# Seven block products instead of eight for half of the hidden features, from batch 2 on

## The chip, the cores and the metric

The kernel runs on one core of one Trainium2 chip. The metric is device microseconds of one execution; less is better. The kernel before took 519.63 us, the median of three runs (519.27 to 521.14).

The core's engines work side by side, each on a queue of its own in a fixed order: TensorE (PE, matrix products, results in the eight PSUM banks), VectorE (DVE), ScalarE (ACT), GpSimd (POOL, which works on SBUF tiles only here) and SyncE (SP), which issues the DMAs.

## The reference, cut to what matters

```
a    = softmax(phi over the sequence)              # per batch and head, 576 x 32
k_m  = einsum('bhsm,bhsd->bhmd', a, k);  v_m = einsum('bhsm,bhsd->bhmd', a, v)
attn = softmax(scale * q @ k_m^T) @ v_m            # 8 batches, 8 heads, 576 tokens, 64 wide
x    = attn, heads side by side                    # 4608 x 512
a, b = x @ w1, x @ w2                              # 512 -> 1024 each
out  = ((a * b) @ w3) @ w_out                      # 1024 -> 1024 -> 512
```

The inputs are float64 words, which the kernel turns into fp32 itself; it works at fp32 accuracy.

## The kernel before, in words

The product w3 @ w_out is made once. Per batch, `v_m` is multiplied into w1 and w2 (`memory_weights`, tokens M0 to M3, one for each quarter of 256 of the 1024 features), so that a and b come from the probabilities directly: the inner dimension is 256 (8 heads x 32 memory slots), in two blocks t of 128. Every operand is split into a high and a low part of reduced width, and a product is three matmuls: high by high, high by low, low by high.

A batch has three stages on PE:

- **a and b** (`ab_unit`, L589). For each half n of the tokens (288) and each f of eight blocks of 128 features, one unit: a in one PSUM bank, b in another, each 2 blocks t x 3 = 6 matmuls of 128x288, so 12 a unit and 16 units, 192 matmuls, a batch. Then ScalarE copies a out of its bank (L609, token `a`), and VectorE multiplies b by it into g (L612, token `g`).
- **sums of g** on GpSimd (L618, L630, L632, L634; tokens f and S), as the out stage already runs on Strassen's scheme in Winograd's form.
- **out** (`out_unit`, L654, token `O`): 14 units of 12 matmuls (L668). For each, ScalarE makes the high part (L646, token h) and VectorE the low part (L652, token l).

The attention of the next batches runs beside this: the softmax of the token scores (scc, mx, sb, ex, sm, mu, tr: L289 to L317), the high and low part of the probabilities `at` (ah L322, al L326), and the matmuls for memories, scores and M (L227, L277, L350), with Mh (ScalarE, L361) and Ml (VectorE, L369).

The order on every engine is written out by hand. The strings FIRST (batch 0), SECOND (batch 1) and BATCH (batches 2 to 7) are lists of tokens, and each engine's queue holds its instructions in the order of the tokens. An engine that reaches an instruction whose input isn't there waits, with all that is queued behind it.

PSUM has four banks `ab` (two pairs, handed out from the list `free_banks`), one pair `o` and one pair `x`. A unit of a and b takes a pair; the bank of a is handed back by ScalarE's copy, the bank of b by VectorE's multiply. So the third unit of a stage needs the first one's multiply.

The SBUF tiles that matter: `ph` (phi transposed), `a` (phi by tokens), `kv0`, `kv2`, `kv4`, `q`, `s_sb` (scores), `at`, one buffer each; `sh` and `sl` (four each), `c` (three).

Of the kernel before, what the change touches and what calls it, by code (L numbers as in the profile page):

```python
# [33 lines left out]
f3 s2 E3 bm g g bs w1 y1 h2 A a A D0 t2 g l2 Et1 E0 S2 z2 be mem A exp norm D1 E1 memc a a l0 g g block O blockc w0
y0 h1 l1 h4 h3 t3 l4 t1 z1 z3 M0 sc0 scc0 mx0 sb0 O O l3 O O Mh0 h6 S3 S1 l6 h5 Ml0 l5 O S4 h7 p4 p1 h11 ex0 l7 O O
h9 h8 C11 sm0 mu0 tr0 l8 sc1 q2 M1 l9 O u2 ah0 h10 l10 O h12 p5 Mh1 h13 scc1 l11 al0 l12 l13 O O O O C21 C22 Ml1 mx1
sb1 ex1 C12 sm1
# [3 lines left out]
be a g A a A mem norm memc g phi2 l0 a A block g a blockc A M0 kv2 a +top g sc0 M1 g scc0 Mh1 f1 h1 A f3 mx0 sb0 A a
f2 a Ml1 ex0 g g sm0 Mh0 A +bm Ml0 a A O a A g h3 h2 +bs l1 g M2 a mu0 l3 +exp +be g sc1 Mh2 S3 l2 M3 scc1 mx1 S2 h4
+mem Ml2 O S1 l4 h5 +norm O p1 O O sb1 ex1 l5 h6 O Mh3 +memc h8 sm1 h7 S4 u2 l6 h9 tr0 O l7 l8 C11 h10 l9 l10 O p5 O
h11 h12 mu1 +block ah0 O O l11 al0 tr1 h13 l13 l12 O q2 C22 C12 +blockc Ml3 ah1 O O al1 C21
# [14 lines left out]
def memory_attention__then__bilinear_ffn_kernel(  # L59
# [84 lines left out]
    def load_phi(b):  # L144
        t = att.tile([P, NT, S], F32, name="ph", tag="ph")
        nc.sync.dma_start(out=t, in_=phiT[b].rearrange("t p s -> p t s"))
        a = att.tile([P, 9 * P], F32, name="a", tag="a")
# [1 line left out]
        loaded["ph", b] = t, a

    def load_kv(b):
        t = []
        for i in range(0, 4, 2):
# [693 lines left out]
```

## Time and profile before

| | |
|---|---|
| median of three runs | 519.63 us |
| the profiled execution | 520.16 us, its span 518.4 us |
| granted TensorE clock | 0.999 of 2.4 GHz |
| PE / DVE / ACT / POOL busy | 507.8 / 383.8 / 279.9 / 149.6 us |

The span runs from the first to the last instruction; 1.8 us of the execution lie around it. Busy time counts the stretches in which at least one instruction of an engine was under way. A matmul's own duration (about 295 ns) overlaps the next one's, so the pace of PE is read from the chain of waits, where a run of matmuls stands with its count.

### The profile page before, as it was taken

What the parts mean: (1) busy time and instruction counts of PE and PEld (TensorE: products, weight loads), DVE (VectorE), ACT (ScalarE), POOL (GpSimd) and SP (SyncE); (2) the same over time, 40 slices, a digit from 0 to 9 for tenths busy, and PEclk for the clock granted to TensorE, in tenths of its full rate; (3) what the DMA queues carried; (4) which work ended last, traced back from release to release, by engine and by line L of the source; (5) the groups of instructions that cost most, each with busy time, mean ns of one, the idle gap of its engine ahead of it and who ended that gap; (6) DMA issues with size and microseconds to landing.
All of it is one profiled execution on the core that took longest, in us unless ns stands there. A gap on an engine that the chain in (4) does not pass through costs nothing.

```text
span 518.4 us, 10996 instructions
## 1 busy us (share of the span) xinstructions
PE 507.8 (98%) x4488; PEld 443.3 (86%) x4488; DVE 383.8 (74%) x647; ACT 279.9 (54%) x494; POOL 149.6 (29%) x158
## 2 busy tenths in 40 slices
PE   7998999999999999999999999999999999999997
PEld 6344459899788998989988998999898989899996
DVE  4878989889869985769566976688577936893363
ACT  6876989864436643645364625373355425543352
POOL 0005005763020801163023602080207111721280
PEclk9999999999999999999999999999999999999999
DMA  8999943603853048004810263006600400010002
GB/s 280 413 406 362 387 172 108 227 1 127 283 189 136 1 161 296 1 2 138 290 31 1 92 229 138 2 4 207 248 1 1 162 24 1 0 60 34 2 3 91
DMA packets 29795, 68.87 MB, mean 133 GB/s; under 512 B 1840, under 2 KB 10032, under 8 KB 29744
## 3 DMA queue, kind: packets, MB, share of 16 engines
q1 hardware_dynamic: 29744, 68.16, 36.9%
q8 instruction: 35, 0.57, 0.5%
q14 instruction: 16, 0.13, 0.1%
HBM read 58.72 MB, written 9.44 MB: 131 GB/s over the span
## 4 chain that ended last, share of the span: by engine, by line
PE 93%; DMA 3%; DVE 1%; issue 1%; ACT 1%; SPq 0%; ACTq 0%; DVEq 0%
PE ab L600 40%; PE o L668 19%; PE x L668 10%; PE ab L668 5%; PE ab L350 3%; PE x L502 3%; PE x L227 3%; DMA raw<-in_w_out 2%; PE o L502 2%; PE ab L502 2%; PE o L350 1%; PE x L350 1%; PE ab L277 1%; DMA raw<-in_w3T 1%; PE x L277 1%
## 5 line engine op out<-in xcount | busy, mean ns | idle before, releaser
L600 PE MATMUL ab<-ah,mh 128*128 128x288 f32 x512 | 152.5, 298 | 0.0
L600 PE MATMUL ab<-al,mh 128*128 128x288 f32 x512 | 151.1, 295 | 1.0 <-DVE al L326 1.0
L600 PE MATMUL ab<-ah,ml 128*128 128x288 f32 x512 | 151.0, 295 | 0.0
L612 DVE TENSOR_TENSOR g<-ab,a_sb 128x288 f32<-128x288 f32 x128 | 57.6, 455 | 71.2 <-PE ab L600 66.3
L609 ACT COPY a_sb<-ab 128x288 f32<-128x288 f32 x128 | 51.2, 401 | 99.5 <-PE ab L600 96.3
L600 PEld LDWEIGHTS ab<-ah,mh 128*128 128x128 f32 x512 | 96.2, 188 | 8.2 <-issue 5.7
L600 PEld LDWEIGHTS ab<-al,mh 128*128 128x128 f32 x512 | 96.3, 188 | 1.5 <-DVE al L326 1.2
L600 PEld LDWEIGHTS ab<-ah,ml 128*128 128x128 f32 x512 | 96.2, 188 | 0.0
L652 DVE TENSOR_TENSOR sl<-g,sh 128x576 fp32r<-128x576 f32 x98 | 83.2, 873 | 6.8 <-ACT sh L646 6.6
L618 POOL TENSOR_TENSOR g<-g,g 128x288 f32<-128x288 f32 x32 | 29.6, 932 | 200.1 <-DVE g L612 200.1
L646 ACT CAST sh<-g 128x576 fp32r<-128x576 f32 x98 | 65.4, 678 | 33.9 <-PE o L668 14.0
L668 PE MATMUL o<-sh,Wh 128*128 128x288 f32 x248 | 74.0, 298 | 0.0
L668 PE MATMUL o<-sh,Wl 128*128 128x288 f32 x248 | 73.2, 295 | 0.0
L668 PE MATMUL o<-sl,Wh 128*128 128x288 f32 x248 | 73.1, 295 | 0.0
L630 POOL TENSOR_TENSOR q<-g,g 128x288 f32<-128x288 f32 x28 | 22.2, 819 | 101.4 <-PE x L277 91.5
L668 PEld LDWEIGHTS o<-sh,Wh 128*128 128x128 f32 x248 | 46.6, 188 | 4.9 <-issue 4.4
L668 PEld LDWEIGHTS o<-sh,Wl 128*128 128x128 f32 x248 | 46.7, 188 | 0.0
L668 PEld LDWEIGHTS o<-sl,Wh 128*128 128x128 f32 x248 | 46.6, 188 | 0.0
L668 PE MATMUL x<-sl,Wh 128*128 128x288 f32 x136 | 40.1, 295 | 0.0
L668 PE MATMUL x<-sh,Wl 128*128 128x288 f32 x136 | 40.1, 295 | 0.0
L668 PE MATMUL x<-sh,Wh 128*128 128x288 f32 x136 | 40.0, 294 | 0.0
L634 POOL TENSOR_TENSOR g<-g,q 128x288 f32<-128x288 f32 x28 | 34.9, 1275 | 0.0
(132 smaller groups left out, 887.2 us busy)
## 6 DMA issues: line engine op xcount, KB each, us to landing
kv<-in_kv SPq DMA_DIRECT2D x16, 1024.0 KB, 9.4
q<-in_qT SPq DMA_DIRECT2D x8, 1152.0 KB, 5.5
outT<-c SPq DMA_DIRECT2D x31, 288.0 KB, 2.4
raw<-in_w3T SPq DMA_DIRECT2D x6, 1024.0 KB, 11.4
ph<-in_phiT SPq DMA_DIRECT2D x8, 576.0 KB, 5.0
a<-in_phi_tok SPq DMA_DIRECT2D x8, 576.0 KB, 5.9
raw<-in_w SPq DMA_DIRECT2D x4, 1024.0 KB, 15.5
kv<-in_w SPq DMA_DIRECT2D x3, 1024.0 KB, 14.3
```

What stands on the lines that cost most here:

```text
L227: nc.tensor.matmul(ps[t][h * M : (h + 1) * M, : 2 * D], lhsT=v["a"][:, (NT * i + t) * P + h * M : (NT * i + t) * P + (h + 1) * M], rhs=kvt ...
L350: nc.tensor.matmul(ps[t][g * M : (g + 1) * M], lhsT=vm[b % 2][d, g], rhs=w12_sb[q][d, :, g], start=True, stop=True,)
L502: nc.tensor.matmul(pw[r][i][:, cols], lhsT=x[:, i * P : (i + 1) * P], rhs=wos[k // half][:, k % half, cols], start=k == 0 and cols.start == 0,
L600: nc.tensor.matmul(banks[w][:, :HALF], lhsT=x[:, t, w, fc : fc + P], rhs=y[:, n, t * HALF : (t + 1) * HALF], start=i == 0, stop=i == len(t ...
L609: nc.scalar.copy(out=a_sb, in_=banks[0][:, :HALF])
L612: nc.vector.tensor_tensor(out=G[n, f // half][:, f % half], in0=banks[1][:, :HALF], in1=a_sb, op=ALU.mult)
L618: nc.gpsimd.tensor_tensor(out=low, in0=top, in1=low, op=ALU.subtract)
L630: gp(out=s2, in0=a22, in1=s3, op=ALU.subtract)
L634: gp(out=a12, in0=a12, in1=s2, op=ALU.subtract)
L646: nc.scalar.copy(out=hi, in_=src)
L652: nc.vector.tensor_tensor(out=lo, in0=src, in1=hi.bitcast(F32), op=ALU.subtract)
L668: nc.tensor.matmul(ps[j][:, :HALF], lhsT=piece(x, s, 2 * part + k)[:, jc], rhs=y[:, k], start=i in first and part == 0 and k == 0 and t == ...
```

## The change

In batches 2 to 7 the last two quarters of the features (f 4 to 7) are no longer made by `ab_unit`. A quarter's a and b together are, for each of w1 and w2, a product of 2 x 2 blocks (2 feature blocks, 2 inner blocks t, 2 token halves). It is now made by seven block products P1 to P7 in place of eight (`block_product`), six matmuls each, so 84 a batch for the two quarters in place of 96.

What goes with it:

- on the weights' side: token Q (in batch 1, once for each of the two quarters) takes differences within `w12_sb`, so that M yields a difference; Mr (ScalarE), Ms (three subtractions or additions on VectorE), Mt (ScalarE) and Mu (VectorE) make three more sums of a quarter and their high and low parts;
- on the probabilities' side: T1 to T4 (GpSimd) replace the blocks of `at` by differences, in place; Th (ScalarE) and Tl (VectorE) make the high and low parts;
- behind the products: k (ScalarE) copies a bank out while it goes on being summed into, e (VectorE) adds a kept part to a bank, and of the four products a times b of a quarter three are made on GpSimd (v1, v2, v4) and one on VectorE (v3, after the copy e30);
- tiles share buffers: `s_sb` takes the buffer of `ph`, `kvm` that of `kv4`, the sums of quarter 2 that of `kv0`, the sums' fp32 form a part of `q`. The load of phi is split in two (phi, tok), the load of kv into kvx (kv2, kv4) and kvy (kv0);
- `memories` adds up its blocks in the order 2, 3, 0, 1; SECOND and BATCH are written in another order.

```diff
 BATCH = """
-A phi2 a A g A a g a A g a +top A a A g g +bm a h0 A +bs g a g M0 sc0 l0 M1 +exp scc0 A a g mx0 A a Mh1 Mh0 g Ml1 A
+phi2 A A a a g -T1 A g A a a -T3 A g -T2 a g -Th1 -Tl1 A g +top tok2 -T4 -Th0 A a -Tl0 h0 h1 g a +bm +exp kvx2 f0
++bs A l0 a M0 Mh0 sc0 M1 g g Mh1 scc0 P1 P5 k10 k11 P6 k50 k20 k21 Ml0 f3 Ml1 P2 mx0 k51 sb0 e11 f2 e10 P3 e21 P7 v1
...
         def sub_max():
+            v["a"] = loaded.pop(("a", b))
...
-                for i in range(4):
+                for i in (2, 3, 0, 1):
...
-            v["kvm"] = att.tile([P, NT, 2 * D], F32, name="kvm")
+            x = att.tile([P, NG * 2 * D], F32, name="kvm", tag="kv4")
+            v["kvm"] = x[:, : NT * 2 * D].rearrange("p (t x) -> p t x", t=NT)
...
+                s_sb = att.tile([P, NT, S], F32, name="s_sb", tag="ph")
...
+        def prob_sums(i):
+            (x11, x21), (x12, x22) = [[v["at"][:, n, t * HALF : (t + 1) * HALF] for t in range(NT)] for n in range(2)]
+            out, in0, in1 = {1: (x11, x12, x11), 3: (x12, x22, x12), 2: (x22, x22, x11), 4: (x21, x21, x22)}[i]
+            nc.gpsimd.tensor_tensor(out=out, in0=in0, in1=in1, op=ALU.subtract)
...
+        def block_sums(tmp, q):
+            p0, p1 = (x.rearrange("p (w f) -> p w f", w=2) for x in ms["ps", q][:2])
+            x11, s3, x12, x22 = p0[:, :, :P], p0[:, :, P:], p1[:, :, :P], p1[:, :, P:]
+            if ("tmp", q) not in ms:
+                ms["tmp", q] = tmp
+                nc.scalar.copy(out=tmp[:, 0], in_=s3)
+                return
+            for j, x, y, op in ((1, x22, 0, ALU.subtract), (0, x11, 1, ALU.add), (2, x12, 1, ALU.subtract)):
+                nc.vector.tensor_tensor(out=tmp[:, j], in0=x, in1=tmp[:, y], op=op)
...
+    def block_product(b, i, q, G):
+        (ah, al), (mh, ml), (sh, sl) = ready["A", b], ready["M", b][q], ready["M", b]["sums", q]
+        t, u = {1: (0, 0), 2: (1, 0), 4: (1, 1), 7: (0, 1), 5: (None, 0), 6: (None, 1), 3: (None, 2)}[i]
...
+        bank = {2: "beta", 5: "gamma", 3: "gamma"}.get(i, "alpha")
+        if i in (1, 2, 5):
+            G[bank, q] = pair_x() if i == 2 else pair_o() if i == 5 and q == NQ - 1 else pair_ab()
+        for w in range(2):
+            for k, (x, y) in enumerate(((0, 0), (0, 1), (1, 0))):
+                nc.tensor.matmul(
+                    G[bank, q][w][:, :HALF],
+                    lhsT=xs[x][:, w],
+                    rhs=ys[y],
...
+    def block_keep(i, w, q, G):
+        if ("kept", i, q) not in G:
+            G["kept", i, q] = big.tile([P, 2, HALF], F32, name="c", tag="c", bufs=3)
+        nc.scalar.copy(out=G["kept", i, q][:, w], in_=G["gamma" if i == 5 else "alpha", q][w][:, :HALF])
+
+    def block_result(i, w, q, G):
+        if i == 3:
+            G["a_sb", q] = big.tile([P, HALF], F32, name="a_sb", bufs=2)
+            nc.scalar.copy(out=G["a_sb", q], in_=G["alpha", q][0][:, :HALF])
+            G["alpha", q].done(0)
+            return
+        bank, kept = {1: ("beta", 1), 2: ("gamma", 2), 4: ("alpha", 5)}[i]
+        c = G["kept", kept, q][:, w]
+        nc.vector.tensor_tensor(out=c, in0=G[bank, q][w][:, :HALF], in1=c, op=ALU.add)
+        if i == 2:
+            G[bank, q].done(w)
+
+    def block_g(i, q, G):
+        n, u = (i - 1) % 2, (i - 1) // 2
+        if i == 3:
+            on, x, y = nc.vector, G["alpha", q][1][:, :HALF], G["a_sb", q]
+        else:
+            on = nc.gpsimd
+            x, y = (G["kept", {1: 1, 2: 2, 4: 5}[i], q][:, w] for w in range(2))
+        on.tensor_tensor(out=G[n, 1][:, 2 * (q - NQ + 2) + u], in0=x, in1=y, op=ALU.mult)
...
-            ends = ((2, 4, 6, 8), (4, 6, 8))[min(b, 1)]
+            ends = ((2, 4, 6, 8), (4, 6, 8))[min(b, 1)] if b < FIRST_BLOCKS else (4,)
...
+                elif what == "Q":
+                    x = w12_sb[quarter(what)][D:]
+                    nc.vector.tensor_tensor(out=x[:, :, :, P:], in0=x[:, :, :, :P], in1=x[:, :, :, P:], op=ALU.subtract)
```

VectorE in batch 3 of the kernel before, from the units around M0, M1 and the first scores on. L612 is g, L289 the transposed scores (scc0), L294 and L298 mx0 and sb0, L369 Ml1 (from bank x) and Ml0 (from bank o).

```order
L612 TENSOR_TENSOR g_2209<-ab,a_sb 128x288 x2
L652 TENSOR_TENSOR sl<-g_2207,sh 128x576
L289 STREAM_TRANSPOSE s_sb<-ab 128x288 x2
L612 TENSOR_TENSOR g_2209<-ab,a_sb 128x288
L294 TENSOR_REDUCE st_2397<-s_sb 128x18
L612 TENSOR_TENSOR g_2208<-ab,a_sb 128x288
L369 TENSOR_TENSOR ml_2420<-x,mh_2415 128x1024
L298 TENSOR_TENSOR s_sb<-s_sb,st_2397 128x576
```

The same place in the changed kernel. L667 is g, L300 scc0, L400 Ml0 and Ml1, L305 and L309 mx0 and sb0, L717 the additions e, L767 a low part l.

```order
L667 TENSOR_TENSOR g_2975<-ab,a_sb 128x288 x2
L300 STREAM_TRANSPOSE s_sb<-ab 128x288 x2
L400 TENSOR_TENSOR ml_3217<-o,mh_3159 128x1024
L400 TENSOR_TENSOR ml_3220<-x,mh_3182 128x1024
L305 TENSOR_REDUCE st_3229<-s_sb 128x18
L309 TENSOR_TENSOR s_sb<-s_sb,st_3229 128x576
L717 TENSOR_TENSOR c<-x,c 128x288 x2
L717 TENSOR_TENSOR c<-ab,c 128x288 x4
L767 TENSOR_TENSOR sl<-g_2973,sh 128x576
```

Ml0 and Ml1 stand next to each other behind scc0, and six additions e in the place of the multiplies g.

GpSimd in batch 3 before, and the first of batch 4: f (L618), S2 and S3 (L630), S1 (L632), S4 (L634).

```order
L618 TENSOR_TENSOR g_2932<-g_2930,g_2932 128x288 x4
L630 TENSOR_TENSOR q<-g_2933,g_2932 128x288 x4
L632 TENSOR_TENSOR g_2930<-q,g_2930 128x288 x4
L634 TENSOR_TENSOR g_2931<-g_2931,q 128x288 x4
L618 TENSOR_TENSOR g_3655<-g_3653,g_3655 128x288 x4
```

And in the changed kernel: T1 to T4 (L342), f (L734), and v1, v2, v4 of the two quarters (L728) ahead of the same sums.

```order
L342 TENSOR_TENSOR at<-at 128x288 x4
L734 TENSOR_TENSOR g_2975<-g_2973,g_2975 128x288 x3
L728 TENSOR_TENSOR g_2974<-c 128x288
L728 TENSOR_TENSOR g_2976<-c 128x288 x2
L734 TENSOR_TENSOR g_2975<-g_2973,g_2975 128x288
L728 TENSOR_TENSOR g_2976<-c 128x288 x2
L728 TENSOR_TENSOR g_2974<-c 128x288
L745 TENSOR_TENSOR q<-g_2976,g_2975 128x288 x4
```

GpSimd gets ten more instructions a batch, four ahead of the f's and six between and behind them.

## Rows read from the trace of the kernel before

**Rows 1.** The page: span, and busy time, share and instructions of each engine.

```profile
span 518.4 us, 10996 instructions
PE 507.8 (98%) x4488; PEld 443.3 (86%) x4488; DVE 383.8 (74%) x647; ACT 279.9 (54%) x494; POOL 149.6 (29%) x158
```

**Rows 2.** Chain of waits, share of the span by engine.

```profile
PE 93%; DMA 3%; DVE 1%; issue 1%; ACT 1%; SPq 0%; ACTq 0%; DVEq 0%
```

**Rows 3.** Busy time by stretch: batch 1, batch 3, batch 7 (from its a and b).

```profile
core 0: us, PE busy (x) PEld busy (x) DVE busy (x) ACT busy (x) POOL busy (x), PEclk, DMA share, GB/s
130.56:192.75 62.19, 60.81 (x659) 54.56 (x658) 51.81 (x91) 32.05 (x61) 14.44 (x16) 1.00 0.46 156
303.44:358.77 55.33, 55.33 (x542) 51.70 (x542) 41.04 (x72) 26.56 (x51) 15.99 (x16) 1.00 0.30 108
466.91:518.40 51.49, 47.60 (x360) 47.36 (x359) 21.99 (x35) 18.38 (x36) 16.10 (x16) 0.99 0.09 30
```

**Rows 4.** Chain in order of time, batch 3: start, length, what.

```profile
303.44 9.52 PE ab L600 x72
...
313.18 1.60 PE ab L600 x12
314.77 1.02 PE o L350 x16
315.79 0.48 PE ab L277 x16
316.28 0.86 PE x L350 x16
```

**Rows 5.** VectorE and GpSimd groups of batch 3: busy, mean ns; idle before.

```profile
L652 DVE TENSOR_TENSOR sl<-g,sh 128x576 fp32r<-128x576 f32 x12 | 10.4, 894 | 0.3 <-ACT sh L646 0.3
L612 DVE TENSOR_TENSOR g<-ab,a_sb 128x288 f32<-128x288 f32 x16 | 7.2, 456 | 9.0 <-PE ab L600 9.0
L618 POOL TENSOR_TENSOR g<-g,g 128x288 f32<-128x288 f32 x4 | 3.6, 915 | 24.3 <-DVE g L612 24.3
```

**Rows 6.** Groups of the whole span, shapes apart.

```profile
L326 DVE TENSOR_TENSOR al<-at,ah 128x576 fp32r<-128x576 f32 x16 | 12.0, 751 | 1.1 <-ACT ah L322 0.6
L209 DVE TENSOR_TENSOR a<-a,x 128x1024 f32<-128x1024 f32 x8 | 9.7, 1216 | 5.0 <-PE x L204 5.0
L565 DVE TENSOR_TENSOR sl<-o,raw 128x256 f32<-128x256 f32 x2 | 0.8, 412 | 0.0
L609 ACT COPY a_sb<-ab 128x288 f32<-128x288 f32 x128 | 51.2, 401 | 99.5 <-PE ab L600 96.3 <-DVE g L612 2.8
```

**Rows 7.** VectorE in order of time, batch 3: start, length, what, idle before.

```profile
305.13 0.46 DVE L612 TENSOR_TENSOR g<-ab,a_sb 128x288 f32<-128x288 f32 x1 [0.64 <-PE ab L600]
306.72 0.46 DVE L612 TENSOR_TENSOR g<-ab,a_sb 128x288 f32<-128x288 f32 x1 [1.13 <-PE ab L600]
...
316.38 0.85 DVE L289 STREAM_TRANSPOSE s_sb<-ab 128x288 f32<-128x288 f32 x2
...
319.41 0.74 DVE L294 TENSOR_REDUCE st<-s_sb 128x18 f32<-128x576 f32 x1
...
321.10 1.22 DVE L369 TENSOR_TENSOR ml<-x,mh 128x1024 fp32r<-128x1024 f32 x1
322.24 0.75 DVE L298 TENSOR_TENSOR s_sb<-s_sb,st 128x576 f32<-128x576 f32 x1
...
343.92 3.94 DVE L652 TENSOR_TENSOR sl<-g,sh 128x576 fp32r<-128x576 f32 x3
...
351.95 0.82 DVE L701 TENSOR_TENSOR c<-ab,c 128x288 f32<-128x288 f32 x2
```

**Rows 8.** GpSimd in order of time, batch 3: the first f, and S4.

```profile
312.01 0.81 POOL L618 TENSOR_TENSOR g<-g,g 128x288 f32<-128x288 f32 x1 [18.82 <-DVE g L612]
...
343.34 5.19 POOL L634 TENSOR_TENSOR g<-g,q 128x288 f32<-128x288 f32 x4
```

**Rows 9.** DMA issues: count, KB each, median us to landing.

```profile
kv<-in_kv SPq DMA_DIRECT2D x16, 1024.0 KB, 9.4
ph<-in_phiT SPq DMA_DIRECT2D x8, 576.0 KB, 5.0
```

More of the change, by code (lines that the diff above doesn't have):

```diff
@@ L26 @@
 C1 C1 C3 C2 C2 C4 C3 C4 C5 C1 C3 C5 C1 C2 C4 C2 C3 C4 C5 C5 C1 C2 C3 C4 C1 C5 C2 C3 C3 C1 C4 C5 C2 C2 C2 C4 C4 C1 C5
-C1 C3 C2 C3 C5 C1 C3 C4 C4 C5 C1 C2 C3 C4 C5 C5 C2 C4 C1 C3 C5 phi0 kv0 C1 C1 C2 C3 C2 q0 X0 X1 X2 W01 C3 C4 C4 C5
-C5 W02 W03 W04 W05 W06 C2 C1 C1 C4 C2 C4 W07 C3 C2 C3 -top C5 K1 -exp C5 -bm -bs W10 Kh1 K3 C4 -norm C1 K0 -be C3
+C1 C3 C2 C3 C5 C1 C3 C4 C4 C5 C1 C2 C3 C4 C5 C5 C2 C4 C1 C3 C5 phi0 tok0 kv0 C1 C1 C2 C3 C2 q0 X0 X1 X2 W01 C3 C4 C4
+C5 C5 W02 W03 W04 W05 W06 C2 C1 C1 C4 C2 C4 W07 C3 C2 C3 -top C5 K1 -exp C5 -bm -bs W10 Kh1 K3 C4 -norm C1 K0 -be C3
@@ L34 @@
[L34 to L37, printed above, removed]
+-mu1 -tr1 C1 -ah0 -al0 W12 W13 W14 W15 W16 M0 Mh0 M1 C3 -ah1 Mh1 C2 W17 C4 Ml0 Ml1 Dt0 C4 A a -al1 g phi1 tok1 A A
+C2 a C3 a Et0 Dt3 g C5 g s3 f0 C1 C5 A A t0 Kh2 Kl2 a a g Et3 C2 M2 Mh2 Dt2 Dt1 g Ml2 A a A C1 C4 g f1 F3 F2 F0 a
@@ L38 @@
+top g C3 r2 q1 A a A C1 a C5 g g C3 C4 C5 kv1 F1 f2 z0 A A D2 a a Kl0 D3 w2 y2 M3 Mh3 g g E2 Et2 Ml3 w3 A A h0 a a
+Kl3 y3 f3 s2 E3 bm g g bs w1 y1 h2 A a A D0 t2 g l2 Et1 E0 S2 z2 be mem A exp norm D1 E1 memc a a l0 g g block O
+blockc w0 y0 h1 l1 h4 h3 t3 l4 t1 z1 z3 M0 sc0 scc0 mx0 sb0 O O l3 O O Mh0 h6 S3 S1 l6 h5 Ml0 l5 O S4 h7 p4 p1 h11
+ex0 l7 O O h9 h8 C11 sm0 mu0 tr0 l8 sc1 q2 M1 l9 O u2 ah0 h10 l10 O h12 p5 Mh1 h13 scc1 l11 al0 l12 l13 O O O O C21
+C22 Ml1 mx1 sb1 ex1 C12 sm1
 """
 SECOND = """
-A a A -mu1 g -tr1 a -M3 g -M2 phi1 A -ah1 top -al1 a kv1 -Mh3 A -Ml3 a -Mh2 h0 g g -Ml2 A a g bm f0 exp bs A a g A
@@ L41 @@
[L41 to L44, printed above, removed]
+tok1 A -mu1 a -tr1 A a -ah1 g g A -M3 -al1 -Mh3 -M2 -Ml3 a g A a phi1 g A h0 a A top exp g a bm bs -Mh2 kv1 A g Q A
@@ L45 @@
+be a phi2 -Ml2 norm g h1 a mem memc Q A g block blockc A a f2 g +top a sc0 +exp g M0 h2 scc0 Mh0 l2 mx0 M1 A a Mh1 g
+A A f1 a a l0 Ml1 sb0 g l1 ex0 tok2 A g Ml0 A +norm a +bm g a A O sm0 f3 +bs h3 f0 a l3 g sc1 kv2 g M2 scc1 +be M3
+mu0 Mr Mh2 S3 +mem Ml2 Ms Mt O h5 tr0 ah0 S2 h4 Mu +memc O p1 l4 S1 l5 h6 O S4 h9 l6 O mx1 Mr h7 O h8 l7 Ms u2 l8 O
+h10 l10 sb1 Mt l9 Mh3 Mu ex1 O O q2 sm1 h11 p5 h13 O h12 C22 l11 mu1 O O l12 C11 l13 Ml3 al0 tr1 O +block +blockc
+ah1 O C12 C21 al1
 """
 BATCH = """
-A phi2 a A g A a g a A g a +top A a A g g +bm a h0 A +bs g a g M0 sc0 l0 M1 +exp scc0 A a g mx0 A a Mh1 Mh0 g Ml1 A
@@ L48 @@
-a A f0 +be sb0 g a kv2 A ex0 a g A g Ml0 h2 f2 h1 A a g O a A l1 g sm0 h3 l3 A a g mu0 +mem sc1 f3 +norm a l2 M3 g
-f1 M2 S2 scc1 Mh3 Mh2 tr0 S3 Ml2 O h9 S1 h4 O mx1 +memc O p1 l4 O h5 l5 S4 O h6 h7 sb1 l6 h8 O l7 O ex1 l8 u2 sm1
-h10 l9 l10 q2 p5 mu1 O h12 O h11 ah0 O l11 O C11 C22 h13 +block l13 l12 O al0 tr1 ah1 O C12 al1 Ml3 +blockc C21
+phi2 A A a a g -T1 A g A a a -T3 A g -T2 a g -Th1 -Tl1 A g +top tok2 -T4 -Th0 A a -Tl0 h0 h1 g a +bm +exp kvx2 f0
++bs A l0 a M0 Mh0 sc0 M1 g g Mh1 scc0 P1 P5 k10 k11 P6 k50 k20 k21 Ml0 f3 Ml1 P2 mx0 k51 sb0 e11 f2 e10 P3 e21 P7 v1
@@ L51 @@
+e20 P5 v2 P1 k10 e41 k11 e40 v4 P4 l1 k51 k50 P6 f1 kvy2 P3 +norm k20 k21 e20 e30 P7 e21 P2 e40 v2 ex0 e41 e10 e11
+P4 v3 sm0 O +be h2 e30 M2 v4 Mh2 v3 v1 mu0 h3 l2 sc1 Ml2 M3 +mem Mr O S2 S3 Ms l3 h4 tr0 p1 scc1 O h5 S1 +memc O S4
+l4 h8 Mt ah0 l5 mx1 O C11 O h6 Mh3 h7 h9 l6 l7 Ml3 u2 l8 O O l9 h10 p5 Mu O +block Mr l10 Ms h12 h11 l11 O C22 O l12
+O h13 al0 Mt O sb1 l13 ex1 Mu sm1 mu1 q2 tr1 C12 +blockc O C21 ah1 al1
 """
@@ L146, in load_phi, with load_tok, load_kv @@
         nc.sync.dma_start(out=t, in_=phiT[b].rearrange("t p s -> p t s"))
+        loaded["ph", b] = t
+    def load_tok(b):
         a = att.tile([P, 9 * P], F32, name="a", tag="a")
         nc.sync.dma_start(out=a, in_=phi_tok[b])
[L149 to L153, printed above, removed]
+        loaded["a", b] = a
+    def load_kv(b, parts=(0, 2, 4)):
+        t = loaded.setdefault(("kv", b), {})
+        for i in parts[: len(parts) - (4 in parts)]:
             x = att.tile([P, 2, 8 * 2 * D], F32, name=f"kv{i}", tag=f"kv{i}")
@@ L156, in load_kv @@
             nc.sync.dma_start(out=x, in_=src)
-            t += [x[:, j] for j in range(2)]
+            t |= {i + j: x[:, j] for j in range(2)}
+        if 4 not in parts:
+            return
         x = att.tile([P, NG * 2 * D], F32, name="kv4", tag="kv4")
@@ L162, in load_kv @@
             nc.sync.dma_start(out=x[j * D : (j + 1) * D], in_=src)
-        loaded["kv", b] = [*t, x]
+        t[4] = x
     def load_q(b):
@@ L168, in load_q @@
         loaded["q", b] = t
-    LOADS = {"phi": load_phi, "kv": load_kv, "q": load_q}
+    LOADS = {"phi": load_phi, "tok": load_tok, "kv": load_kv, "kvx": lambda b: load_kv(b, (2, 4)), "kvy": lambda b: load_kv(b, (0,)), "q": load_q}
     def load(what, b):
@@ L183, in top @@
         def top():
-            v["ph"], v["a"] = loaded.pop(("ph", b))
+            v["ph"] = loaded.pop(("ph", b))
             v["mx"] = att.tile([P, NT], F32, name="mx")
@@ L230, in memories @@
                             rhs=kvt[i][:, (4 * t + h) * 2 * D : (4 * t + h + 1) * 2 * D],
-                            start=i == 0,
+                            start=i == 2,
                             stop=False,
@@ L286, in tokens_down @@
             ps, nb = v["scores", n], NBLK // 2
+            if "s" not in v:
+                s_sb = att.tile([P, NT, S], F32, name="s_sb", tag="ph")
+                v["s"] = s_sb.rearrange("p n (k m) -> p n k m", m=M)
             for t in range(NT):
@@ L335, in attention @@
             steps |= {f"{name}{n}": lambda bank, f=f, n=n: f(n) for n in range(2)}
+        steps |= {f"T{i}": lambda bank, i=i: prob_sums(i) for i in range(1, 5)}
+        steps |= {f"Th{n}": lambda bank, n=n: sums_high(n) for n in range(2)}
+        steps |= {f"Tl{n}": lambda bank, n=n: sums_low(n) for n in range(2)}
         return steps
@@ L371, in low, with block_high, block_low @@
             ms[q].append(ml)
+        def block_sums(tmp, q):
[7 more added lines that the diff above has]
+                nc.vector.tensor_tensor(out=tmp[:, j], in0=x, in1=tmp[:, y], op=op)
+        def block_high(q):
+            if q == NQ - 1:
+                ms["sums", q] = [big.tile([P, 3, 2, P], F32R, name=f"ms{x}", tag=f"ms{x}") for x in "hl"]
+            else:
+                x = att.tile([P, 2, 8 * 2 * D], F32R, name="ms", tag="kv0")
+                ms["sums", q] = [x[:, i, : 6 * P].rearrange("p (j w f) -> p j w f", j=3, w=2) for i in range(2)]
+            nc.scalar.copy(out=ms["sums", q][0], in_=ms["tmp", q])
+        def block_low(q):
+            hi, lo = ms["sums", q]
+            nc.vector.tensor_tensor(out=lo, in0=ms["tmp", q], in1=hi.bitcast(F32), op=ALU.subtract)
         steps = {f"M{q}": lambda bank, q=q: step(q, bank) for q in range(NQ)}
+        steps |= {x: lambda bank, q: block_sums(bank(), q) for x in ("Mr", "Ms")}
+        steps |= {"Mt": lambda bank, q: block_high(q), "Mu": lambda bank, q: block_low(q)}
         steps |= {f"Mh{q}": lambda bank, q=q: high(q) for q in range(NQ)}
@@ L614, in ab_unit, with spare @@
         yield
+    FIRST_BLOCKS = 2
+    def spare(G):
+        if "spare" not in G:
+            x = att.tile([P, NG, S], F32, name="q", tag="q").rearrange("p g s -> p (g s)")
+            G["spare"] = x[:, half * HALF : half * HALF + 6 * P].rearrange("p (j w f) -> p j w f", j=3, w=2)
+            G["S2"] = x[:, : half * HALF].rearrange("p (k s) -> p k s", k=half)
+        return G["spare"]
+    def block_product(b, i, q, G):
+        (ah, al), (mh, ml), (sh, sl) = ready["A", b], ready["M", b][q], ready["M", b]["sums", q]
+        t, u = {1: (0, 0), 2: (1, 0), 4: (1, 1), 7: (0, 1), 5: (None, 0), 6: (None, 1), 3: (None, 2)}[i]
+        xs = [m[:, t, :, u * P : (u + 1) * P] for m in (mh, ml)] if t is not None else [m[:, u] for m in (sh, sl)]
+        if i < 4:
+            n, t = {1: (0, 0), 2: (0, 1), 3: (1, 1)}[i]
+            ys = [y[:, n, t * HALF : (t + 1) * HALF] for y in (ah, al)]
+        else:
+            n, j = {5: (0, 0), 4: (0, 1), 7: (1, 0), 6: (1, 1)}[i]
+            ys = [y[:, j] for y in ready["T", b][n]]
+        bank = {2: "beta", 5: "gamma", 3: "gamma"}.get(i, "alpha")
[7 more added lines that the diff above has]
+                    rhs=ys[y],
+                    start=i in (1, 2, 5) and k == 0,
+                    stop=i in (2, 3, 4) and k == 2,
+                    skip_group_check=True,
+                )
@@ L616, in first_sum @@
+    def block_g(i, q, G):
+        n, u = (i - 1) % 2, (i - 1) // 2
+        if i == 3:
+            on, x, y = nc.vector, G["alpha", q][1][:, :HALF], G["a_sb", q]
+        else:
+            on = nc.gpsimd
+            x, y = (G["kept", {1: 1, 2: 2, 4: 5}[i], q][:, w] for w in range(2))
+        on.tensor_tensor(out=G[n, 1][:, 2 * (q - NQ + 2) + u], in0=x, in1=y, op=ALU.mult)
+        if i == 3:
+            G["alpha", q].done(1)
     def first_sum(k, G):
@@ L625, in sums @@
             if "S2" not in G:
-                x = att.tile([P, NG, S], F32, name="q", tag="q")
-                G["S2"] = x.rearrange("p g s -> p (g s)")[:, : half * HALF].rearrange("p (k s) -> p k s", k=half)
+                spare(G)
             s2 = G["S2"][:, k]
@@ L747, in batches, with quarter @@
             n_o = 0
+            seen = {}
+            def quarter(what):
+                seen[what] = seen.get(what, 0) + 1
+                return NQ - 3 + seen[what]
             for what in tokens((FIRST, SECOND, BATCH)[min(b, 2)]):
@@ L772, in batches @@
                         steps[at][what.lstrip("-")](memory_bank(b, in_a, what))
+                elif key in ("Mr", "Ms", "Mt", "Mu"):
+                    if b + 1 < B:
+                        steps[b + 1][what](lambda: spare(G), quarter(what))
+                elif key == "P":
+                    block_product(b, int(digit), quarter(what), G)
+                elif key == "k":
+                    block_keep(int(digit[0]), int(digit[1]), quarter(what), G)
+                elif key == "e":
+                    block_result(int(digit[0]), int(digit[1]), quarter(what), G)
+                elif key == "v":
+                    block_g(int(digit), quarter(what), G)
+                elif what == "Q":
+                    x = w12_sb[quarter(what)][D:]
+                    nc.vector.tensor_tensor(out=x[:, :, :, P:], in0=x[:, :, :, :P], in1=x[:, :, :, P:], op=ALU.subtract)
                 elif key == "W":
```

16 lines of the change are left out of this document (11 added, 5 removed).

## The prediction

> **What bounds the kernel now.** I read the page first: PE is busy for 507.8 of 518.4 us, VectorE for 383.8, ScalarE for 279.9, GpSimd for 149.6 [rows 1]. Since a matmul's busy time is modelled, the second view is the chain of waits: 93% of it is PE itself, 3% DMA, 1% VectorE [rows 2]. Then the stretches. In batch 3 PE is busy for all of 55.33 us, in batch 1 for 60.81 of 62.19 [rows 3]. So in the steady batches nothing makes PE wait, and a matmul taken away is time saved, so long as no other engine takes PE's place. The candidate is VectorE: 41.04 us busy in a batch of 55.33, 14.3 idle. ScalarE has 26.56, GpSimd 15.99.
>
> **What is removed.** In the chain 72 matmuls of a and b take 9.52 us [rows 4], 132.2 ns each. Seven products of 6 for eight make 84 matmuls a batch out of 96: 12 fewer, 1.59 us, and in six batches 72 fewer, **9.5 us**. The block products have the same shape (128x128 by 128x288), so I give them the same pace. M, the scores, the memories and out keep their number of matmuls. With nothing lost, 520.16 of the profiled execution (span 518.4 and 1.8 around it) becomes 510.6; the median of the runs lies 0.5 lower, so 510.1 on that scale.
>
> **What is added to VectorE**, per batch. Twelve e's and two v3 take the place of 8 g's. A single PSUM addition of this shape takes 0.456 [rows 5], two in a row 0.82 [rows 7], so some 0.41 when nothing waits: 14 x 0.41 = 5.7 less 8 x 0.456 = 3.6, +2.1. Two low parts Tl as al, 0.751 [rows 6]: +1.5. Six of Ms on 128x256 from PSUM, like the subtraction of 0.412 [rows 6]: +2.5. Two Mu on 128x768 aren't in the trace: between al (576 columns, 0.75) and the addition on 1024 columns (1.22) [rows 6]; I take 0.95, +1.9. Sum +8.0, so 49 us of work in a batch that PE could do in 55.33 - 1.59 = 53.74. It fits, with 4.7 us idle where there were 14.3. In batch 7 nothing of the next batch's M is made, so there is room.
>
> ScalarE gets 12 more instructions a batch (six k's and the copy e30 a quarter for four a's, two Th, and Mr and Mt twice): 12 at 0.4 to 0.9 are 5 to 11 us on 26.56, hidden in a batch of 53.7. GpSimd gets ten, at 0.81 [rows 8] 8.1 on 15.99, hidden as time of its own.
>
> **Where VectorE's smaller reserve meets PE.** The dense place is the stage of block products. Counted from a batch's start: 8 units and the transposes, 12.9 us, then M0, scores and M1 (1.02, 0.48, 0.86 [rows 4]), so P1 starts at 15.3. The scores end at 14.4; scc0 begins 0.1 later and takes 0.85 [rows 4, 7], done at 15.4. Behind it now stand Ml0 and Ml1, 1.22 each, which were spread between multiplies before: done at 17.8. P2 is the next writer of bank x, which Ml1 reads, and PE reaches it after P1, P5, P6, 18 matmuls, at 17.7: late by 0.1 to 0.2. Then mx0 and sb0 (0.74 and 0.75 [rows 7]), 19.3, and six e's at 0.41: the fourth, which frees the pair that the second quarter's P1 takes, ends at 20.9, where PE is there at 15.3 + 42 x 0.132 = 20.8; the sixth, for which P4 waits, at 21.8 against 21.6. So VectorE is about level with PE, late by 0.1 to 0.3 once; what has been lost is not lost twice, since PE's delay lets VectorE catch up. Then it waits for the second quarter (P3 ends at 24.2). I price this stage at **0.3 us a batch, 1.8 in six**. Its bounds: 0, and 1.6 a batch (below, second rival).
>
> The other tight place is the batch's end. VectorE goes there through the low parts, Ms, Mu, sm1, mu1, tr1, C12, km, vm and al1, and the next batch's first multiply stands behind them. Before, it was idle 0.64 ahead of that multiply, and 1.13 ahead of the second [rows 7]. With 8.0 more work I sum it to some 2.5 us behind the start of the batch. The first multiply frees the bank for the second half of the third unit, at 30 matmuls, 3.97 us; 2.5 + 0.46 is ahead of that. So I cost it at nothing, with 1 us of cover.
>
> **Batch 1** prepares batch 2: two subtractions Q (1024 columns, at most the 1.22 of the addition), six of Ms, two Mu, 2.4 + 2.5 + 1.9 = 6.8 on VectorE, which there has 62.19 - 51.81 = 10.4 idle [rows 3] and PE already lost 1.4. Its order is rewritten, too. Bounds: -1.4 (PE's idle time goes) to +3.6 (6.8 of work where only 3.2 of the idle time can be filled). I take **+0.7**, nearer to no loss, since the idle time there is larger than the work.
>
> **The shared buffers** cost nothing. Phi's load waits for tr1 now (as `s_sb` lies in its buffer), some 0 to 1 us into the batch; 5.0 to land [rows 9], and top stands behind five g's at 8. On SP the second half of phi and kvx stand behind it, which are wanted from 11 and 30 us on. kvy (1 MB) waits until the first quarter's P3 has read the sums in `kv0`, at 19; even with the 9.4 of a load beside others [rows 9] it is there at 29, and the memories, which start with blocks 2 and 3, come to it at 31. Behind it on SP stands only C11's store, at 38. Late by more than 2 us it would stop PE. q's load waits for the second Mu; behind it are C12's and C21's stores and the next phi.
>
> **Sum.** -9.5 + 1.8 + 0.7 = -7.0: 513.2 for the profiled execution, **512.6** on the scale of the median.
>
> **The rivals.**
>
> *Nothing is lost.* The P stage and batch 1 keep PE fed: 510.1, or 509.5 if batch 1 loses less than before. For it: the steady batches now have not one idle stretch of PE that another engine ends, and my lateness is within the error of 0.1 us a step. Against: VectorE's reserve falls from 14.3 to 4.7.
>
> *The hand-offs of the banks cost a step each.* In the P stage PE adds to a bank after ScalarE (k) or VectorE (e) has read it: P6, P7, P3, P4, eight times a batch. A hand-off takes the pipeline's 0.16 us beyond the last matmul's issue, the copy 0.40 [rows 6], and is covered by the one product between (0.79). Where ScalarE is still at another instruction (Mh1, 1 us, stands ahead of k10) or a kept buffer `c` waits for GpSimd's v, the cover is gone; at 0.2 a hand-off this is 1.6 a batch, 9.5 in six, the whole gain: **519.6**. In between, half of it is 515.
>
> *VectorE sets the pace.* Of its 14.3 us idle, 9.0 are waits for PE ahead of the 16 multiplies [rows 5]; if its waits for PE stay at 4.5 for the eight units that are left and 4 to 5 more in the new stage, 49 of work and 9 of waits are 58 a batch, 2.7 over the 55.33 of now, in batches 2 to 6 13 us, less 1.6 in batch 7: about **531**. It decides from waits above 6.3 us a batch on (55.33 - 49). What can raise the work is GpSimd: in rows 7 and 8 three low parts take 3.94 us where four subtractions on GpSimd take 5.19; alone they would be some 0.75 and 0.81 each, 5.5 together, so the two go one after the other. With ten more GpSimd instructions, most of which run beside e and g (one input of those in PSUM), I count four meetings, up to 3 us a batch, and 52 is still under 53.74.
>
> The Trainium skill states this as a rule ("SBUF — State Buffer", section "Who interferes with whom"): a VectorE instruction with two SBUF inputs and a GpSimd instruction that reads SBUF exclude each other for their whole length. The trace agrees, by the 3.94 and 5.19. If all ten met such an instruction, VectorE would be at 57 of 53.7 and the kernel slower; the rule itself says that e, g and Ml, with one input in PSUM, don't meet them.
>
> **How the numbers follow.** The forecast's mechanism (511 to 515) 0.58; nothing lost 0.20; hand-offs (515 to 522) 0.15; VectorE sets the pace 0.07. A measurement of this kernel can tell about 0.5%, 2.6 us, from no change: faster is below 517.0, slower above 522.2. Faster: 0.58 + 0.20 + 0.07 of the hand-offs' 0.15 = 0.85. Same: the other 0.08. Slower: 0.07. The range runs from 509.3 (nothing lost, batch 1 mended) to 517.0; what is left out is the upper half of the hand-offs and VectorE's pace, 0.15.
>
> **What would show it.** The chain of waits should hold 42 matmuls of a quarter at 132 ns; gaps ahead of P2, the second P1 or P4 with VectorE as releaser show my 0.3, gaps ahead of P6, P7 or P3 with ScalarE as releaser the hand-offs. A steady batch should be 54.0 us, with VectorE busy for 49 to 51. If batch 3 is 55 or more, with waits of a and b's third unit for VectorE's multiply, the batch's end was what I sized wrongly; if the memories wait for a DMA of kv, the late load.

## The result, and the profile after

The changed kernel took 514.35 us (median of four runs, 513.46 to 514.89) against 520.04 for the kernel before (four runs): a ratio of 0.9887, 95% interval 0.9862 to 0.9913. The forecast was 512.6, within 509.3 to 517.0. The profiled execution took 513.95 us, 6.2 less than the one shown ahead of the prediction; its span is 6.4 shorter.

The page's head and the shares of the chain of waits, after, beside [rows 1, 2]:

```profile
span 512.0 us, 11116 instructions
PE 502.0 (98%) x4416; PEld 434.3 (85%) x4416; DVE 426.1 (83%) x745; ACT 310.1 (61%) x566; POOL 198.1 (39%) x218
PE 87%; DVE 7%; DMA 4%; issue 1%; ACT 1%; SPq 0%; ACTq 0%; DVEq 0%
```

PE has its 72 matmuls fewer (4488 before). VectorE stood for 1% of the chain and now for 7%: there are places where PE waits for it. The 7% is not what these waits cost: at the start of batches 3 to 6 PE stops for 0.34 us, and the chain then follows VectorE's work back for 8.9 us (batch 4: from 302.75 to 293.86). Busy time by stretch, from the first matmul of a and b of one batch to that of the next (batch 1 is counted from where the chain has its start, 0.16 behind the start of its first matmul, in every kernel here): batch 1, a steady batch (4), and batch 7 to the end of the span.

```profile
core 0: us, PE busy (x) PEld busy (x) DVE busy (x) ACT busy (x) POOL busy (x), PEclk, DMA share, GB/s
130.37:191.16 60.79, 60.76 (x658) 54.74 (x656) 54.80 (x95) 33.50 (x64) 16.77 (x16) 1.00 0.45 156
300.03:354.67 54.64, 54.42 (x530) 50.14 (x529) 47.09 (x87) 31.61 (x63) 23.49 (x26) 1.00 0.33 109
461.60:512.00 50.40, 46.53 (x350) 46.05 (x348) 30.54 (x46) 21.82 (x45) 25.42 (x26) 0.98 0.10 36
```

(Batches are counted from 0; the steady stretch of [rows 3] is batch 4 as well, which ahead of the prediction is called batch 3. Steady batches read alike. Batch 1 in [rows 3] also ends where the chain has the next batch's start: 62.19 there, 62.03 below.) From such starts, in each kernel's trace, the lengths of the batches; batch 7 ends with the start of its last matmul:

| us | 1 | 2 | 3 | 4 | 5 | 6 | 7 |
|---|---|---|---|---|---|---|---|
| before | 62.03 | 55.34 | 55.34 | 55.34 | 55.35 | 52.79 | 47.47 |
| after | 60.79 | 54.23 | 54.64 | 54.64 | 54.63 | 52.30 | 46.27 |
| less | 1.24 | 1.11 | 0.70 | 0.70 | 0.72 | 0.49 | 1.20 |

Batches 2 to 7 are 4.9 us shorter where 72 matmuls alone would make 9.5; batch 1, which has as many matmuls as before, is 1.2 shorter. The chain of waits in the product stage of batch 4 (start, length, what):

```profile
315.89 2.58 PE ab L695 x18
318.48 0.04 issue
318.52 1.06 PE x L695 x6
319.58 1.59 PE ab L695 x12
321.18 0.80 PE o L695 x6
321.97 2.39 PE ab L695 x18
324.36 0.80 PE o L695 x6
325.16 0.80 PE ab L695 x6
```

From 319.58 on the matmuls follow at 132 to 133 ns; ahead of them P2 (`x`) is held up, and its 6 take 1.06 instead of 0.79. VectorE at that place:

```profile
315.39 0.83 DVE L300 STREAM_TRANSPOSE s_sb<-ab 128x288 f32<-128x288 f32 x2
316.15 1.18 DVE L400 TENSOR_TENSOR ml<-o,mh 128x1024 fp32r<-128x1024 f32 x1
317.26 1.21 DVE L400 TENSOR_TENSOR ml<-x,mh 128x1024 fp32r<-128x1024 f32 x1
318.39 0.73 DVE L305 TENSOR_REDUCE st<-s_sb 128x18 f32<-128x576 f32 x1
319.16 0.76 DVE L309 TENSOR_TENSOR s_sb<-s_sb,st 128x576 f32<-128x576 f32 x1
```

P2 starts 0.05 behind the end of Ml1 (the second L400), which reads bank x. And PE at the start of batch 5, where one matmul stands 0.47 behind the one ahead of it, instead of 0.13:

```profile
356.92 0.29 PE L655 MATMUL ab<-ah,ml 128*128 128x288 f32 x1
357.39 0.37 PE L655 MATMUL ab<-ah,mh 128*128 128x288 f32 x1 [0.18 <-DVE vm L274]
357.60 0.29 PE L655 MATMUL ab<-al,mh 128*128 128x288 f32 x1
```

It is the second half of the second unit, held up by the copy vm, which with km is the last reader of the bank that held `blocks` (km and vm are VectorE's copies of a later batch's k_m and v_m out of PSUM). VectorE there, vm, the low part al1 and the batch's first multiply g:

```profile
356.96 0.28 DVE L274 COPY vm<-ab 64x128 f32<-64x128 f32 x1
357.17 0.74 DVE L337 TENSOR_TENSOR al<-at,ah 128x576 fp32r<-128x576 f32 x1
357.83 0.44 DVE L667 TENSOR_TENSOR g<-ab,a_sb 128x288 f32<-128x288 f32 x1
```

### The profile page after: what moved, and what is told of

Same layout as the page of the kernel before. It is cut to its first block, busy times and chain, and to the rows that moved or that the text cites. A ratio compares the mean times of both kernels' runs of the same rounds, so it can differ in the third digit from the quotient of the medians.

```text
span 512.0 us, 11116 instructions
## 1 busy us (share of the span) xinstructions
PE 502.0 (98%) x4416; PEld 434.3 (85%) x4416; DVE 426.1 (83%) x745; ACT 310.1 (61%) x566; POOL 198.1 (39%) x218
## 4 chain that ended last, share of the span: by engine, by line
PE 87%; DVE 7%; DMA 4%; issue 1%; ACT 1%; SPq 0%; ACTq 0%; DVEq 0%
PE ab L655 23%; PE o L783 17%; PE ab L695 10%; PE x L783 8%; PE ab L783 5%; PE ab L381 3%; PE ab L557 3%; PE x L557 3%; PE x L236 3%; DMA raw<-in_w_out 2%; PE o L557 2%; PE x L695 2%; PE o L695 2%; PE o L381 1%; PE x L381 1%; DVE c L816 1%
## 5 line engine op out<-in xcount | busy, mean ns | idle before, releaser
L655 PE MATMUL ab<-ah,mh 128*128 128x288 f32 x320 | 96.1, 300 | 0.7 <-DVE vm L274 0.7
L655 PE MATMUL ab<-al,mh 128*128 128x288 f32 x320 | 94.4, 295 | 0.0
L655 PE MATMUL ab<-ah,ml 128*128 128x288 f32 x320 | 94.4, 295 | 0.0
L767 DVE TENSOR_TENSOR sl<-g,sh 128x576 fp32r<-128x576 f32 x98 | 84.2, 871 | 7.2 <-ACT sh L761 6.7
L734 POOL TENSOR_TENSOR g<-g,g 128x288 f32<-128x288 f32 x32 | 28.3, 895 | 104.0 <-DVE g L667 104.0
L655 PEld LDWEIGHTS ab<-ah,mh 128*128 128x128 f32 x320 | 60.1, 188 | 5.7 <-PE ab L655 1.5
L655 PEld LDWEIGHTS ab<-al,mh 128*128 128x128 f32 x320 | 60.2, 188 | 0.2 <-issue 0.2
L655 PEld LDWEIGHTS ab<-ah,ml 128*128 128x128 f32 x320 | 60.2, 188 | 0.0
L664 ACT COPY a_sb<-ab 128x288 f32<-128x288 f32 x80 | 31.8, 398 | 36.3 <-PE ab L655 35.3
L342 POOL TENSOR_TENSOR at<-at 128x288 f32<-128x288 f32 x24 | 19.4, 808 | 84.7 <-DVE at L328 75.5
L667 DVE TENSOR_TENSOR g<-ab,a_sb 128x288 f32<-128x288 f32 x80 | 35.6, 452 | 19.2 <-PE ab L655 18.7
L728 POOL TENSOR_TENSOR g<-c 128x288 f32<-128x288 f32 x36 | 31.2, 893 | 32.2 <-DVE c L717 32.2
```

Source lines behind the costliest of these rows:

```text
L342: nc.gpsimd.tensor_tensor(out=out, in0=in0, in1=in1, op=ALU.subtract)
L655: nc.tensor.matmul(banks[w][:, :HALF], lhsT=x[:, t, w, fc : fc + P], rhs=y[:, n, t * HALF : (t + 1) * HALF], start=i == 0, stop=i == len(t ...
L664: nc.scalar.copy(out=a_sb, in_=banks[0][:, :HALF])
L667: nc.vector.tensor_tensor(out=G[n, f // half][:, f % half], in0=banks[1][:, :HALF], in1=a_sb, op=ALU.mult)
L728: on.tensor_tensor(out=G[n, 1][:, 2 * (q - NQ + 2) + u], in0=x, in1=y, op=ALU.mult)
L767: nc.vector.tensor_tensor(out=lo, in0=src, in1=hi.bitcast(F32), op=ALU.subtract)
```

## The experiments

**km and vm earlier (e1).** Theory A: PE waits for particular readers of banks, and each wait can be lifted by itself. Rival B: VectorE sets the pace, and the bank is only where it shows.

```diff
-ex1 Mu sm1 mu1 q2 tr1 C12 +blockc O C21 ah1 al1
+ex1 Mu +blockc sm1 mu1 q2 tr1 C12 O C21 ah1 al1
```

> The changed kernel, but token +blockc (km and vm, 4 instructions, 1.1 us on VectorE) stands ahead of sm1, mu1, tr1, C12 instead of behind them. Theory A (the batch's second unit takes the PSUM bank that km and vm read, and waits for them: 0.34 us at the start of batches 3 to 6): those four waits go, the batches 3 to 5 go from 54.63 to 54.3 us, the span from 512.0 to 510.6, the time down by 1.4 us. Rival B (VectorE sets the pace at the batch's end, the bank is only where it shows): the first multiply g is late instead, the third unit waits, and time and batches stay within 0.3 us.

Measured 513.07 us, ratio to the kernel before 0.9882 (0.9866 to 0.9897). The intervals of the two ratios overlap, so the verdict is the trace's: batch 3 (from 246.00) went from 54.64 to 54.23,

```profile
246.00:300.23 54.23, 54.18 (x531) 50.11 (x530) 47.20 (x87) 31.53 (x63) 23.51 (x26) 1.00 0.33 110
```

and batches 4, 5 and 6 became 54.33, 54.22 and 51.89: 0.3 to 0.4 less each, with VectorE as busy as before and no wait at the start of a batch. Theory A; B fell. The span, 511.1, shrank by less than the batches, since the part ahead of batch 2 was 0.6 longer in this execution; it varies so between executions (below).

**M1 ahead of M0 (e2), and both (e3).**

```diff
-M0 Mh0 sc0 M1 g g Mh1 scc0 ... Ml0 f3 Ml1 P2
+M1 Mh1 sc0 M0 g g Mh0 scc0 ... Ml1 f3 Ml0 P2
```

> The changed kernel, but in batches 2 to 7 M1 (bank x) is made ahead of M0 (bank o) and its low part first on VectorE. Theory A (P2 writes bank x, which Ml1 reads last: 0.2 to 0.3 us a batch in batches 2 to 6): the wait ahead of P2 goes, P5 of the second quarter, the next writer of o, has time, batches 2 to 6 are 0.25 us shorter, the time 1.2 us. Rival B (VectorE sets the pace of the whole stage of products): the wait goes to the second P1 or P4 instead, time unchanged within 0.3 us. Rival C (the gap is the change of shape from M to products and not a wait): gap and time unchanged.

> Both edits of the two runs before at once: km and vm earlier, M1 ahead of M0. Theory A: the two waits are independent, 1.4 + 1.2 = 2.6 us less than the changed kernel, span 509.4, steady batches 54.05 us. Rival B: VectorE has the pace, one of the two waits comes back elsewhere, under 1.4 us less.

Measured 515.18 us, ratio 0.9916 (0.9902 to 0.9929), and 512.98, ratio 0.9877 (0.9864 to 0.9891). In e2 that is none of its three forecasts. In e2 batch 4 is 54.83, longer by 0.2. VectorE and PE at M's start, e2:

```profile
315.03 0.58 DVE L222 TENSOR_TENSOR a<-a,x 64x128 f32<-64x128 f32 x2
315.75 1.09 PE L381 MATMUL x<-w,vm 64*32 64x512 f32 x16 [0.44 <-DVE a L222]
```

The wait ahead of P2 is gone, but M1, now first, finds bank x still read by sub_max (token bs), the maxima of phi that were transposed into it: PE stands for 0.44 us there. The same in e3, 0.45, and its batch 4 is 54.43. e3 is 1.4 us below the changed kernel, the edge of what its rival B had named, but the wait that it has left is the one that M1 brought with it. So my edit had a wait of its own, and says nothing on B.

**Ml1 ahead of Ml0 (e7),** on top of e1. The order on PE stays; on VectorE mx0 fills the time until Mh1 is there.

```diff
-Ml0 f3 Ml1 P2 mx0 k51 sb0
+mx0 f3 Ml1 P2 Ml0 k51 sb0
```

> The kernel with km and vm earlier (e1), and the order of M0 and M1 on PE as in the changed kernel, but on VectorE the low part Ml1 (bank x) stands ahead of Ml0 (bank o), with mx0 between scc0 and Ml1 while ScalarE makes Mh1. M1 is no longer made early, so it doesn't meet the transposed maxima that VectorE still reads from bank x. Theory A (P2 waits for Ml1 alone, 0.32 us a batch): the wait goes, batches 2 to 6 are 0.3 us shorter than in e1 (steady ones 53.9), batch 7 the same, the time 1.5 us less, 511.5. Rival B (VectorE sets the pace of the stage): the wait turns up ahead of P4 or the second P1 and the time stays within 0.4 us of 513.1.

Measured 512.45 us, ratio 0.9863 (0.9844 to 0.9882), the lowest of all; batches 2 to 5 are 54.04, 54.03, 54.04, 54.04, 0.2 to 0.3 less than in e1, batch 7 the same. A was right on the place and too high on the size: it had 53.9 for a steady batch and 511.5 in all, and batch 6 did not get shorter (51.92, 51.89 in e1). The intervals of e1 and e7 overlap, so this verdict, too, is the trace's. The product stage, e7:

```profile
315.08 2.58 PE ab L695 x18
317.67 0.92 PE x L695 x6
318.58 1.59 PE ab L695 x12
320.17 0.80 PE o L695 x6
320.97 2.40 PE ab L695 x18
```

The stop ahead of P2 is gone (0.1 of it stays, at which no engine is named) and has not come back at P4 or the second P1. Theory A again. A steady batch is 0.60 shorter than in the changed kernel, by two moves that take nothing off VectorE.

**v1, v2, v4 on VectorE (e4).**

```diff
-            on = nc.gpsimd
+            on = nc.vector
```

> The changed kernel, but v1, v2 and v4 (six multiplies of 128x288 a batch, from SBUF) are made on VectorE instead of GpSimd, at the same place in the order. Theory A (VectorE is about level with PE in the stage of products and at the batch's end): 6 x 0.4 = 2.4 us more work on it delays the second P1 and P4 by 0.4 to 0.8 us a batch and the batch's end by 0.5 to 1.5: batches 3 to 5 are 1 to 2 us longer, the time 6 to 12 us more than the changed kernel. Rival B (VectorE is idle for 7.5 us of a batch and has reserve): under 0.3 us a batch, under 2 us in all.

Measured 520.49 us, ratio 1.0017 (1.0008 to 1.0027): 6.1 more than the changed kernel, all the gain. Batch 4, and PE at P4:

```profile
302.22:357.72 55.50, 54.95 (x530) 50.20 (x529) 49.61 (x93) 31.85 (x63) 18.74 (x20) 1.00 0.31 107
```

```profile
324.67 0.29 PE L695 MATMUL ab<-ah,ml 128*128 128x288 f32 x1
325.22 0.40 PE L695 MATMUL ab<-sh,mh 128*128 128x288 f32 x1 [0.26 <-DVE c L717]
```

VectorE has 2.5 us more work a batch and is still idle for 5.9, and yet the batch is 0.86 longer (below the 1 to 2 expected) and batch 7, 47.63, 1.36. The additions e come late for P4, by 0.42 in the first quarter and 0.23 in the second; in out a high part by ScalarE comes late in batch 6 (0.48, at 447.26) and a low part in batch 7 (0.80, at 495.77). So in the product stage VectorE is level with PE, and GpSimd's share of a times b is what keeps it there; B fell.

**Eight products (e5).** The first product of each quarter is made twice.

```diff
-        for w in range(2):
+        for w in [0, 1] * (1 + (i == 1)):
```

> The changed kernel, but the first product P1 of each quarter is made twice (6 matmuls more, added to the same bank), so that PE has its 12 matmuls a batch back, and all the rest of the change stays; what is computed is then wrong by one product. Theory A (the gain is PE's 12 matmuls a batch, 1.59 us, less waits for VectorE of 0.3 ahead of P2 and 0.34 at the batch's start, which the longer stage hides): batch 2 and 7 longer by 1.3 to 1.6, 3 to 6 by 0.9 to 1.3, the time 6.5 to 8 us more than the changed kernel, at or above the kernel before. Rival B (VectorE sets the pace): the 12 matmuls are hidden behind VectorE, under 3 us more. Rival C (what the change gained comes from the rewritten order, not from the matmuls): under 3 us more, too, with batches 2 and 7 unchanged.

Measured 522.73 us, ratio 1.0059 (1.0044 to 1.0073), 8.4 more than the changed kernel, just above what A expected. Batch 4 is 55.92, 1.28 more: 12 matmuls, 1.59, less the 0.3 of P2's wait, which is gone: with P1 made twice, Ml1 is done when P2 comes. Batch 7, where P2 doesn't wait, is 1.60 more. So a matmul less is worth its 132 ns, and with P1 made twice the kernel is slower than the one before: B and C fell.

**al1 ahead of top in the kernel before (e6).**

```diff
-phi1 A -ah1 top -al1 a kv1
+phi1 A -ah1 -al1 top a kv1
```

> The kernel before, but in batch 1 the low part al1 stands ahead of top on VectorE (one swap in SECOND). In the kernel before top waits 2.4 us for a load of phi there and PE then waits 1.2 us for al1; in the changed kernel batch 1 is 1.2 us shorter. Theory A (that part of the gain is the new order of al1 and top alone, not block products): batch 1 goes from 62.2 to about 61.0 us, the time down by 1.2 us. Rival B (the load of phi or the work behind is late anyway): top and what hangs on it come late, PE waits elsewhere in batch 1, time unchanged within 0.3.

Measured 518.83 us, ratio to the kernel before 0.9987 (0.9978 to 0.9996). Batch 1, then VectorE in it:

```profile
130.10:190.84 60.74, 60.37 (x658) 54.34 (x657) 51.76 (x91) 32.07 (x61) 14.45 (x16) 1.00 0.46 159
```

```profile
135.64 0.76 DVE L326 TENSOR_TENSOR al<-at,ah 128x576 fp32r<-128x576 f32 x1 [0.40 <-ACT ah L322]
136.89 1.35 DVE L186 TENSOR_REDUCE mx<-ph 128x2 f32<-128x1152 f32 x1 [0.49 <-DMA ph<-in_phiT]
```

Batch 1 is 1.29 shorter than before and as long as in the changed kernel (60.79), and the batches behind it are as before. The swap alone gives it. (The medians differ by 0.8, where 1.2 was expected.) The same place in the kernel before, VectorE and PE:

```profile
138.06 1.35 DVE L186 TENSOR_REDUCE mx<-ph 128x2 f32<-128x1152 f32 x1 [2.36 <-DMA ph<-in_phiT]
140.13 0.40 PE L600 MATMUL ab<-al,mh 128*128 128x288 f32 x1 [1.02 <-DVE al L326]
```

## Why the prediction was right

The time lay 1.8 us from the forecast and inside the range; the profiled execution, 513.95, is 0.8 above the sum's 513.2. The matmuls and the wait in the product stage were right; that the sum came so near is in part luck, since two errors in it, 2.8 and 1.9 us, offset each other.

**The 9.5 us of matmuls** stand: e5 gives 1.60 for 12 where nothing else waits, against 1.59.

**The product stage, 0.3 a batch:** right in place and size, in four batches instead of six (1.2 us for the 1.8). Ml1, moved behind scc0 and Ml0, holds up P2 by 0.3 in batches 2 to 5 (e7 gives 0.2 of it back, 0.1 stays); the second P1 and P4 come out just in time, and e4 shows how close. In batches 6 and 7, where VectorE has less to do, P2 doesn't wait.

**VectorE's work** I put at +8.0 a batch; it is 47.09 - 41.04 = 6.05. What was added is nearly what I summed. What had been there before became shorter: the 14 low parts of out take 11.5 us for 12.4 (12 of them 819 ns each, 894 before [rows 5]), and two subtractions sb 1.5 for 2.1; they met GpSimd less often, whose sums end at 42.8 us of batch 4 instead of 45.3. The e's cost 0.39 each in a row (four in 1.54); the single 0.456 of [rows 5] that I took for an addition is a multiply.

**The batch's end, "I cost it at nothing": this step failed.** VectorE was further behind than I summed: I had it through the whole list, al1 included, at some 2.5 us; vm ends 2.57 us into batch 5 (357.24), and the first multiply begins at 3.16. Still, that multiply, which the third unit needs at 3.97 us, ends in time, at 3.60, with 0.4 of cover instead of 1. I looked at the wrong reader. The bank of `blocks`, the last to be handed back, goes to the second unit, which wants it after 18 matmuls, at 2.4; its readers km and vm stood behind sm1, mu1, tr1 and C12. That is 0.3 to 0.4 in batches 3 to 6, which e1 gives back.

**Batch 1, +0.7 taken, -1.2 measured,** within its bounds, but of the wrong sign. Of the 1.4 us that PE lost there 1.3 was al1 standing behind top, which waited for phi's load; the new order lifted it (e6). The preparation of the sums costs batch 1 nothing that can be seen.

**Batches 6 and 7** I gave the steady price. Batch 6 lost 1.1 of its 1.59, 0.4 by km and vm. It has no memories to make for a later batch (2.27 us of PE), so PE comes to out earlier while, as I read it, Ms and the low parts are where they were (no run tried this):

```profile
440.35 1.78 PE o L783 x12
442.13 3.35 PE ab L783 x24
445.49 3.22 PE o L783 x24
448.70 3.36 PE x L783 x24
```

24 matmuls take 3.17 elsewhere. In batch 7 GpSimd's sums now run further into out, to 14.3 us behind the last product (499.92; before, to 10.2 behind the last matmul of a and b), and the low parts, one after the other with them, slow down:

```profile
490.62 4.16 POOL L747 TENSOR_TENSOR g<-q,g 128x288 f32<-128x288 f32 x4
494.73 5.19 POOL L749 TENSOR_TENSOR g<-g,q 128x288 f32<-128x288 f32 x4
```

```profile
492.49 0.81 DVE L816 TENSOR_TENSOR c<-ab,c 128x288 f32<-128x288 f32 x2
493.98 6.56 DVE L767 TENSOR_TENSOR sl<-g,sh 128x576 fp32r<-128x576 f32 x5 [0.68 <-ACT sh L761]
```

1.31 us each; alone they take 0.75, and the three in a row of the kernel before take 0.99 (502.43). C11's addition, with one input in PSUM, keeps its length beside GpSimd (two in 0.81, at 492.49), as the rule weighed in the prediction (the Trainium skill, "SBUF — State Buffer", "Who interferes with whom") has it.

**The account.** 9.5 less 4.9 leaves 4.6 lost in batches 2 to 7: P2 4 x 0.3 and the batch's start 4 x 0.4, read from the chain and given back by e7 (0.2 of the 0.3) and e1 (all); some 0.9 in out of batches 6 and 7, read from the chain; the remaining 0.9, some 0.15 a batch, I put down to M2, which now stands behind out matmuls and takes 1.02 instead of 0.86. That wasn't tried. M2 and M3 in batch 4, before and after:

```profile
335.95 1.72 PE ab L350 x32
```

```profile
329.15 1.02 PE ab L381 x16
330.17 0.48 PE x L285 x16
330.66 0.86 PE ab L381 x16
```

I had said 1.8; the 2.8 more are offset by batch 1's 1.9.

**The rivals.** "Nothing is lost" is what e7 comes near to in steady batches (54.04, against 53.74 without a wait). The hand-offs by ScalarE cost nothing to be seen: no wait of a product names a k. VectorE's pace was no bound on the whole batch, with 7.5 us idle, and was one on single banks. The late load of `kv0` stopped nothing.

## What to carry to other kernels

When work moves from the full engine to one that has reserve, don't compare sums over a stage: list the banks and buffers that the full engine writes next, in its order, and for each where its last reader stands in the other engine's queue. Two moves of such readers gave 0.6 us a batch here without taking away any work. And a rewritten order should be measured apart from what it was rewritten for; of the 6.4 us gained in the span, 1.2 came from one swap that the kernel before could have had.
